# Attention of 32 heads as float32 products of whole operands, two heads side by side on TensorE, in a kernel with two mixture-of-experts layers behind it

## The chip, the core and the metric

The kernel runs on one core of a Trainium2 chip, as one launch. The core has five engines that the text names: TensorE (PE: matrix products; its weight loads are listed apart as PEld), VectorE (DVE), ScalarE (ACT), GpSimd (POOL) and SyncE (SP), which here only issues DMAs. TensorE reads SBUF and writes PSUM; GpSimd works on SBUF alone. The metric is the device time of one execution in microseconds; the median of the runs counts. Every engine works through its own instructions in the order in which the program was written out, and waits where a semaphore tells it to.

## What is computed

Attention over 4 batches of 8 heads, with 576 tokens of 64 numbers each; then a top-1 layer of 8 experts on the 2304 tokens of 512 numbers, then a second such layer, all in float32.

```python
def _attn_ref(q, k, v, tau):
    scale = 1.0 / np.sqrt(q.shape[-1])
    scores = scale * np.matmul(q, k.transpose(0, 1, 3, 2))
    thresh = np.max(scores, axis=-1, keepdims=True) - tau
    scores = np.where(scores >= thresh, scores, -1000000000.0)
    scores = scores - np.max(scores, axis=-1, keepdims=True)
    attn = np.exp(scores)
    attn = attn / (np.sum(attn, axis=-1, keepdims=True) + 1e-09)
    return np.matmul(attn, v).astype(np.float32)
...
x = attn_out.transpose(0, 2, 1, 3).reshape(B * S, H * D)
x = _moe_ref(x=x, **moe_kwargs)          # expert of the largest cosine with expert_emb
return _moe2_ref(x=x, **moe2_kwargs)     # expert of the largest x @ w_gate
# each: out = gate * (relu(x[mask] @ w1[e]) @ w2[e]), e by e
```

## The kernel before

The program has two parts, one after the other. `Attn` does the 32 heads in 16 pairs (heads A and B of a pair); `Moe` then does the two layers of experts. The change touches `Attn` alone.

**The work of a pair.** A head's 576 query tokens are four tiles of 128 rows and 64 tokens left over; the leftovers of both heads share a ninth row tile, R. Row tiles 0 to 3 are of head A, 4 to 7 of head B, 8 is R. For each row tile `scores` (L290) makes 128x576 scores in a PSUM tile `S` of two banks (two buffers), and `least` (L308) scales and negates them into SBUF on VectorE and takes the row's least. Then a row tile goes one of two ways. Five of the nine in a pair between the first and the last two (`MASK_LAST`, L134) take the exponential on ScalarE at once (`exp all`, L342) and are masked afterwards by one VectorE instruction that also makes the row's sum (`mask`, L347). The other four get 1e30 where the score is beyond the bound (`beyond`, VectorE, L322), which GpSimd adds to the scores (`add`, L327) before ScalarE's exponential. `bound` (L317) is a small GpSimd sum per two row tiles.

The probabilities are then transposed by TensorE in units (`unit_t`, L361): a head's 512 tokens by 128 keys (four units) or 64 keys (the fifth), and two units for R. The units, multiplied with the values and summed over the keys (`unit_av`, L414), give 64 values by 512 tokens in the PSUM tile `av`. `out_copy` (L436) brings that to SBUF, `out_rows` (L442) turns it into rows of tokens with the head's part of the router's logits, and `out_scale` (L454) divides by the sums and sends the rows to DRAM.

**Products of parts.** A product is not taken of the float32 numbers as they are. Every operand is split into a high part (ScalarE copies it into the shorter float32r format) and a low part (the difference, on VectorE or GpSimd), and the parts' products are summed in PSUM, each a float32r product. For the scores, queries and keys are split (`hi`, `copy`, `lo`, L244 to L268), and eight or more DMAs per pair (`put`, L270) lay the parts out so that [qh; ql] meets [kh; kh] in one product of 128 rows and qh meets kl in a second. For the values, `values_hi` and `values_lo` (L223, L228) split the values, and `unit_hi` and `unit_lo` (L378, L403) every unit; a unit's low part is made by GpSimd for the units named in `POOL_LO`, after another copy by ScalarE (`unit_copy`, L398), and by VectorE for the rest. Two places have undivided float32 products already: the scores of the first pair (L298), and the one unit of a pair named in `NATIVE` (L129), whose product takes 64 of TensorE's 128 columns (L429).

**What sets the order.** `ops` (L480) lists every step of all pairs with its engine, an assumed duration, what it needs and which buffers it takes. `schedule` (L69) plays them through: an engine that is free takes its ready step with the lowest number from the table `PRIO` (L37) plus 9 per pair. The instructions are then written out by the planned start. So the steps of a pair's scores lie among those of the values of the pair before. Steps have names such as `av B3`; the durations in the listing are the planner's and not the chip's.

Of the kernel before, what the change touches and what calls it, by code (L numbers as in the profile page):

```python
# [36 lines left out]
PRIO = {'warm': -10000, 'add': (-0.16, -0.16, -34.65), 'av A0': (-64.69, -36.16, -74.17), 'av A1': (91.89, 55.73, 39.12), 'av A2': (11.55, -7.69, -15.93),  # L37
        'av A3': (-7.31, -19.57, 3.89), 'av A4': (29.52, 7.73, 37.81), 'av B0': (-101.89, -32.26, -71.6), 'av B1': (1.15, -3.58, 51.29), 'av B2': (27.87, 57.62, 70.32),
        'av B3': (16.24, 19.49, -11.83), 'av B4': (-65.09, -76.86, -45.68), 'av R4': (-52.77, -109.13, -78.47), 'beyond': (-27.93, -27.93, -68.77),
        'bound': (32.21, -8.27, -34.63), 'cpk': (-26.19, -26.19, -9.74), 'cpq': (-78.84, -78.84, -72.62), 'emb norm': 63.12, 'emb put': 185.35, 'emb t': -26.7,  # L40
# [4 lines left out]
        'keys first': 6.99, 'ld w1': 9875.33, 'ldk': (-19.25, -19.25, -6.75), 'ldq': (-40.12, -40.12, -34.25), 'ldv': (-1.36, -19.35, -1.74),  # L45
# [3 lines left out]
        'loq': (24.41, 24.41, 13.42), 'mask': (42.11, 16.85, 52.98), 'out copy A': (2.77, -32.01, -26.34), 'out copy B': (-7.87, 4.44, 9.13),  # L49
        'out copy R': (4.59, -18.98, -47.96), 'out rows A': (-58.69, 8.96, 16.81), 'out rows B': (48.05, 22.06, 57.31), 'out rows R': (100.98, 70, 72.19),  # L50
        'out scale A': (58.37, 23.19, 48.16), 'out scale B': (-22.09, -8.89, 10), 'out scale R': (16.66, -68.73, 5.62), 'params': -3.56,
        'put kh': (-34.17, -34.17, -52.2), 'put qh': (-125.91, -125.91, -110.79), 'put ql': (-46.61, -46.61, -81.72), 'queries A': -1.77, 'queries B': -31.15,
        'raw A0': -5.76, 'raw A2': (-19.29, -23.07, -16.97), 'raw A3': (-21.66, -5.31, -11.85), 'raw B2': (-27.43, -44.98, -62.27), 'raw B3': (17.51, 21.04, 11.67),
        'route add': (-28.79, -28.79, -28.09), 'route argmax': (-42.73, -42.73, -64.14), 'route count': (-101.52, -101.52, -16.14), 'route perm': (5.63, 5.63, -18.58),
        'route prefix': (6.1, 6.1, -7.24), 'route slots': (11.96, 11.96, 28.01), 'scores': (4.78, 0.94, 6.14), 'sign': 38.43, 't A0': (-33.6, 6.93, 4.21),
# [65 lines left out]
class Attn:  # L121
    """Attention of the 32 heads, in pairs; rows of values, and logits of the first router, go to DRAM.

    Of a pair of heads A, B, token 4 p + t stands at row p of tile t; the last 64 tokens of both share tile R.
    Scores are three products of exact parts: [qh; ql] [kh; kh] and qh kl; R takes those of both heads, with zeros between.
    Probabilities are masked after the exponential or before it, transposed, and split like the others.
    """
    UNITS = [(h, k) for h in 'AB' for k in range(5)] + [('R', 0), ('R', 4)]  # of a pair's transposed probabilities
    # in the first pair, those between, the last but one, the last  # L129
    NATIVE = [('A', 1)], [('A', 1)], [('A', 1), ('B', 1)], [('A', 1), ('B', 1), ('A', 2)]  # units whose product with the values is a float32 one  # L130
    # units whose low part GpSimd makes
    POOL_LO = [('A', 3), ('B', 3), ('B', 2), ('A', 2)], [('A', 3), ('B', 3), ('B', 2), ('A', 2)], [('A', 3), ('B', 3), ('B', 2), ('A', 2), ('A', 0)], [('A', 3), ('B', 3), ('B', 2)]
# [74 lines left out]
    def emb_put(s): s.nc.vector.tensor_copy(s.ie[:, :, 64:72], s.pe)  # L207
# [272 lines left out]
    def ops(s, params, done):  # L480
        O = []
# [649 lines left out]
```

## Time and profile before

| what | value |
|---|---|
| median of three runs (1127.10 to 1131.44) | 1127.37 us |
| span of the profiled execution | 1131.5 us |
| its instructions | 17365 |
| first and last `least` of the attention | start at 11.5 and 406.8 us |
| last copy of `av`, the end of the attention's products | starts at 425.0 us |
| TensorE busy, of the span | 957.3 us (85%) |
| VectorE | 713.7 us (63%) |
| ScalarE | 543.9 us (48%) |
| GpSimd | 502.5 us (44%) |

The profile is one execution on the chip. Its span runs from the first to the last instruction; of the three timed runs the slowest, 1131.44 us, is nearest to it, and the median lies 4.1 us below. A group of instructions is named by line, engine, operation and the program's tiles (`out<-in`), with the shape; behind it stand the number of instructions, their time together and the mean of one, then the idle time of the engine before them and who ended it. A record of TensorE runs from the entry of the first column to the end of the last, so that successive records overlap: the distance of their starts, not the length of one, is what a product costs. A product of undivided float32 operands leaves two records. "128x512" at the end of a TensorE group is its output, and 128*64 before it says that 128 rows and 64 columns of the array take part.

### The profile page before, as it was taken

The page shows a single profiled execution, that of the slowest core. Times are in us where ns is not written, and L with a number is a line of the kernel's source. Part 1 is how long each engine was busy: PE and PEld are TensorE (multiplying, and loading weights), DVE is VectorE, ACT ScalarE, POOL GpSimd, SP SyncE. Part 2 cuts the span into 40 slices and gives each one's busy share as a digit, 9 for nine tenths or more (in the row PEclk, how much of TensorE's full clock was granted, in tenths as well). Part 3 has the DMA queues.
Part 4 walks back from the last instruction along what each step waited for, and adds up shares of the span by engine and source line. Part 5 has one row for each costly group of instructions (what it writes and reads, how often), then busy time and mean ns, then how long its engine had stood idle before and what let it go on. Part 6 is the DMA issues. An engine that isn't in the chain of part 4 may idle for free. (4 is left out here: it accounts for less than half of the span.)

```text
span 1131.5 us, 17365 instructions
## 1 busy us (share of the span) xinstructions
PE 957.3 (85%) x5685; PEld 831.9 (74%) x5685; DVE 713.7 (63%) x1611; ACT 543.9 (48%) x1019; POOL 502.5 (44%) x551
## 2 busy tenths in 40 slices
PE   7889899987997995897898798968589898879774
PEld 5777677776786774797787787967578887679673
DVE  7899999999798974563566365435434434344430
ACT  5788768875695772452355243322233322333420
POOL 5687768865686653332343334113313322132321
PEclk9999989998897995988999898989699999996998
DMA  6565646644344022644464444214435433364400
GB/s 161 127 146 125 147 107 149 150 116 95 84 110 96 21 68 61 190 123 139 153 188 137 130 156 137 86 46 152 138 102 195 138 105 118 100 198 149 154 17 24
DMA packets 119527, 136.83 MB, mean 121 GB/s; under 512 B 74869, under 2 KB 78965, under 8 KB 119168
## 3 DMA queue, kind: packets, MB, share of 16 engines
q1 hardware_dynamic: 111648, 109.30, 35.5%
q0 software_dynamic: 7520, 23.90, 6.1%
q14 instruction: 274, 2.24, 0.8%
q8 instruction: 85, 1.39, 0.5%
HBM read 95.40 MB, written 16.68 MB: 99 GB/s over the span
## 5 line engine op out<-in xcount | busy, mean ns | idle before, releaser
L851 PE MATMUL l1p<-xh,w1h 128*128 128x256 f32 (+7 forms) x576 | 190.9, 331 | 82.1 <-issue 53.4
L851 PEld LDWEIGHTS l1p<-xh,w1h 128*128 128x128 f32 x576 | 123.2, 214 | 89.5 <-issue 75.6
L851 PE MATMUL l1p<-xl,w1h 128*128 128x256 f32 (+7 forms) x576 | 185.2, 321 | 0.0
L851 PE MATMUL l1p<-xh,w1l 128*128 128x256 f32 (+7 forms) x576 | 184.9, 321 | 0.0
L854 ACT ACTIVATE hh<-l1p 128x256 fp32r<-128x256 f32 (+7 forms) x144 | 57.9, 403 | 191.0 <-PE l1p L851 146.2
L861 PE MATMUL yps<-w2h,hh 128*128 128x512 f32 x344 | 140.2, 408 | 0.0
L861 PE MATMUL yps<-w2l,hh 128*128 128x512 f32 x344 | 134.5, 391 | 0.0
L861 PE MATMUL yps<-w2h,hl 128*128 128x512 f32 x344 | 134.5, 391 | 0.0
L784 DVE TENSOR_TENSOR w2l<-rw,w2h 128x1024 fp32r<-128x1024 f32 x48 | 74.3, 1559 | 94.7 <-issue 42.3
L784 POOL TENSOR_TENSOR w1l<-rw,w1h 128x1024 fp32r<-128x1024 f32 x17 | 50.6, 2975 | 173.4 <-ACT w1h L783 156.5
L851 PEld LDWEIGHTS l1p<-xl,w1h 128*128 128x128 f32 x576 | 123.4, 214 | 0.0
L851 PEld LDWEIGHTS l1p<-xh,w1l 128*128 128x128 f32 x576 | 123.0, 214 | 0.0
L313 DVE TENSOR_SCALAR_CACHE_REDUCE sn<-psS,nsc 128x576 f32<-128x576 f32 x144 | 114.6, 809 | 12.9 <-PE psS L302 6.9
L783 ACT ACTIVATE w2h<-rw 128x1024 fp32r<-128x1024 f32 x64 | 66.0, 1052 | 109.1 <-PE yps L861 53.4
L370 PE MATMUL pt<-ident,p 128*128 128x128 f32 (+1 forms) x640 | 98.5, 287 | 14.0 <-DVE h L412 8.7
L856 DVE SCALAR_TENSOR_TENSOR hl<-l1p,hh 128x256 fp32r<-128x256 f32 (+7 forms) x144 | 62.8, 446 | 69.4 <-ACT hh L854 64.0
L412 POOL TENSOR_TENSOR lo<-raw,hi 128x512 fp32r<-128x512 f32 x64 | 86.5, 1352 | 32.0 <-ACT raw L401 31.6
L329 POOL TENSOR_TENSOR b<-sn,b 128x576 f32<-128x576 f32 x57 | 84.2, 1479 | 32.7 <-DVE b L325 29.9
L370 PEld LDWEIGHTS pt<-ident,p 128*128 128x128 f32 (+1 forms) x640 | 76.0, 141 | 29.4 <-DVE h L412 11.3
L350 DVE SCALAR_TENSOR_TENSOR p<-sn,th,b 128x576 f32<-128x576 f32 x87 | 94.5, 1091 | 1.0 <-ACT b L345 0.8
L393 ACT ACTIVATE hi<-pt 128x512 fp32r<-128x512 f32 x109 | 63.1, 596 | 38.0 <-PE pt L370 36.7
L345 ACT ACTIVATE b<-sn,nm 128x576 f32<-128x576 f32 x87 | 67.5, 776 | 18.0 <-DVE sn L313 16.2
(253 smaller groups left out, 2176.7 us busy)
## 6 DMA issues: line engine op xcount, KB each, us to landing
rw<-in_moe_w_dram SPq DMA_DIRECT2D x128, 512.0 KB, 4.2
KA<-kh SPq DMA_DIRECT2D x30, 144.0 KB, 4.8
KB<-kh SPq DMA_DIRECT2D x30, 144.0 KB, 2.6
rawk<-in_k_dram SPq DMA_DIRECT2D x16, 256.0 KB, 3.5
rawq<-in_q_dram SPq DMA_DIRECT2D x16, 256.0 KB, 3.7
rawv<-in_v_dram SPq DMA_DIRECT2D x16, 256.0 KB, 3.2
xs<-xb SPq DMA_DIRECT2D x16, 256.0 KB, 3.1
sA<-qh SPq DMA_DIRECT2D x15, 144.0 KB, 2.6
```

What stands on the lines that cost most here:

```text
L313: s.nc.vector.tensor_scalar(out=sn, in0=st.pop(('ps', r))[:, 224:800], scalar1=s.scale, scalar2=3e38, op0=ALU.mult, op1=ALU.min, accum_out ...
L329: s.nc.gpsimd.tensor_tensor(out=st['b', r], in0=st.pop(('sn', r)), in1=st['b', r], op=ALU.add)
L345: s.nc.scalar.activation(out=b, in_=st['sn', r], func=AF.Exp, scale=-1.0, bias=s.of(st, 'nm', r))
L350: s.nc.vector.scalar_tensor_tensor(out=p, in0=st.pop(('sn', r)), scalar=s.of(st, 'th', r), in1=st.pop(('b', r)), op0=ALU.is_le, op1=ALU.mu ...
L370: for t in range(4): s.nc.tensor.transpose(pt[0:n, t * 128:t * 128 + 128], st['p', 4 * (h == 'B') + t][:, k * 128:k * 128 + n], s.id)
L393: s.nc.scalar.activation(out=t if o is None else o, in_=pt, func=AF.Copy)
L412: (nc.gpsimd if pool else nc.vector).tensor_tensor(out=lo, in0=pt, in1=hi.bitcast(F32), op=ALU.subtract)
L783: def split_hi(s, W, R, k): s.nc.scalar.activation(out=W[0][k], in_=R[k], func=AF.Copy)
L784: def split_lo(s, W, R, k, eng): eng.tensor_tensor(out=W[1][k], in0=R[k], in1=W[0][k].bitcast(F32), op=ALU.subtract)
L851: s.nc.tensor.matmul(o, s.W1[a][k][:, fs], X[b][:, k, n0:n1], start=(q == 0), stop=(q == 3 * KC - 1))
L856: s.nc.vector.scalar_tensor_tensor(out=s.H[1][f][:, n0:n1], in0=o, scalar=0.0, in1=s.H[0][f][:, n0:n1].bitcast(F32), op0=ALU.max, op1=ALU. ...
L861: s.nc.tensor.matmul(ps, s.H[a][f][:, ts], s.W2[b][f // 2][:, f % 2, :], start=(f == 0 and q == 0), stop=(f == FC - 1 and q == 2))
```

## The change

Operands are no longer split anywhere in the attention. Queries and keys are transposed, copied once (keys by VectorE, queries by ScalarE) and used as they are: `Tq` and `Tk` hold head A in partitions 0 to 63 and head B in 64 to 127. Row tiles are numbered anew: 2t is tile t of head A, 2t+1 of head B. A step `scores t` makes both, and takes both buffers of `S`: for each half of the keys a product of head A, which uses TensorE's rows 0 to 63, and one of head B, which uses rows 64 to 127. For tile R the queries are laid out with zeros, so that one product of 128 rows serves both heads.

With the values, each unit is copied from PSUM once, by ScalarE, and `av k` takes the units of both heads: head A's product uses TensorE's columns 0 to 63 and writes partitions 0 to 63 of `av`, head B's the other half. The values are used as they were loaded. The units of 64 keys became units of 128 with the last 64 keys in their lower half and zeros in the values for the rest. `out_copy` and `out_rows` then work on both heads together: four products of 144 columns take the place of eight of 72.

What falls away: all steps `hi`, `lo`, `raw`, `put`, `vh` and `vl`, and the first pair's own products. New are `cpk` on VectorE, zeros that are set once in the buffers of queries and values, and one more DMA for the queries' last tokens (one less for the values). Six row tiles of a middle pair are masked after the exponential and three before it (`MASK_FIRST`); in the first and the last two pairs all nine after it. The table `PRIO` is replaced by one of times within a pair, with 17 per pair. The part with the experts is untouched.

```diff
+    MASK_FIRST = (), (2, 4, 6), ()
...
+    def copy(s, j, nm):
...
+        if nm == 'q': s.nc.scalar.activation(out=st['Tq'], in_=st['psq'], func=AF.Copy)
+        else: s.nc.vector.tensor_copy(st['Tk'], st['psk'])
...
-                nc.tensor.matmul(o, st['S' + h][:, c:c + 128], st['K' + h][:, ks], start=True, stop=False)
-                nc.tensor.matmul(o, st['H' + h][:, t:t + 128], st['kl'][:, ks], start=False, stop=True)
...
+    def scores(s, j, t):
+        nc, st = s.nc, s.pair[j]
+        q, k = st['Tq'], st['Tk']
+        rr = (2 * t, 2 * t + 1) if t < 4 else (8,)
+        for r in rr: st['ps', r] = s.psS.tile([128, 1024], F32, tag='S', name='psS')
+        for i in range(2):
+            ks = slice(i * 288, i * 288 + 288)
+            for h, r in enumerate(rr):
+                p = slice(64 * h, 64 * h + 64) if t < 4 else slice(0, 128)
+                nc.tensor.matmul(st['ps', r][:, (224, 512)[i]:(512, 800)[i]], q[p, 128 * t:128 * t + 128], k[p, ks], start=True, stop=True)
...
     def unit_copy(s, j, u):
...
+        if u in s.of_pair(s.DVE_COPY, j): s.nc.vector.tensor_copy(t, pt)
+        else: s.nc.scalar.activation(out=t, in_=pt, func=AF.Copy)
...
+    def unit_av(s, j, k):
...
+        if k == 'R':
...
+            for k in range(5):
+                for i in range(2):
+                    p = t[:, 128 * k:128 * k + 128] if k < 4 else r
+                    nc.tensor.matmul(av[64 * i:64 * i + 64], v(i, k), p[:, 64 * i:64 * i + 64], start=(k == 0), stop=(k == 4))
             return
-        i = int(h == 'B')
         if k == 0: st['av'] = s.psA.tile([128, 512], F32, tag='av', name='av')
-        av = st['av']
-        if s.native(j, u): nc.tensor.matmul(av[0:64], st['rawv'][:, i * 320 + k * 64:i * 320 + k * 64 + 64], p, start=False, stop=False)
-        elif k < 4:
-            nc.tensor.matmul(av, v(i, k), p[0], start=(k == 0), stop=False)
-            nc.tensor.matmul(av, v(i, k), p[1], start=False, stop=False)
-        else: nc.tensor.matmul(av, v(i, 4), p, start=False, stop=True)
...
+        for i, h in enumerate('AB'):
+            nc.tensor.matmul(st['av'][64 * i:64 * i + 64], v(i, k), st.pop(('u', (h, k))), start=(k == 0), stop=(k == 4))
...
-                    if r in s.of_pair(s.MASK_LAST, j):
-                        x = op('exp all', j, 'A', .76, step(s.exp_all), [least[r]], r, alloc=['b'])
...
+                    if r not in s.of_pair(s.MASK_FIRST, j):
+                        x = op(f'exp all {r}', j, 'A', .70, step(s.exp_all), [l], r, alloc=['b'])
...
-        caps = dict(S=2, T=2, A=1, M=1, rawk=2, rawq=2, rawv=3, nat=2, kh=2, qh=2, tr=2, kl=2, ql=2, KA=2, SA=2, V=3, sn=4, b=3, P=12, hi=3, lo=3, h4=2, r4=2, rhl=1, avs=2, avsR=1, xb=2)
+        caps = dict(S=2, T=2, A=1, M=1, rawk=2, rawq=2, rawv=3, Tk=2, Tq=2, sn=5, b=3, P=14, u=6, r4=2, avsM=2, avsR=2, xb=2)
```

The first place is TensorE's row of work in the middle of an early pair of the kernel before: one native unit (L429), the transpose of R's unit of 64 keys and those of a head's unit (L367, L370), a unit's two products with the values (L431, L432) and one row tile's scores (L301, L302, head B).

```order
L429 MATMUL av<-raw,rawv 64x512
L367 MATMUL pt<-ident,p 64x128
L431 MATMUL av<-hi,Nv 128x512
L432 MATMUL av<-lo,Nv 128x512
L370 MATMUL pt<-ident,p 128x128 x4
L301 MATMUL psS<-KB,sB_190 128x288
L302 MATMUL psS<-kl,hB_194 128x288
L301 MATMUL psS<-KB,sB_190 128x288
L302 MATMUL psS<-kl,hB_194 128x288
```

The same place of the changed kernel: L321 are the two heads' products of one `av k`, L232 the four products of one `scores t`, L295 the transposes of units (four make one).

```order
L321 MATMUL av<-u,rawv_182 64x512 x2
L232 MATMUL psS<-Tk,Tq 128x288 x4
L295 MATMUL pt<-ident,p 128x128 x8
L321 MATMUL av<-u,rawv_182 64x512 x2
L232 MATMUL psS<-Tk,Tq 128x288 x4
L295 MATMUL pt<-ident,p 128x128 x8
L321 MATMUL av<-u,rawv_182 64x512 x2
L295 MATMUL pt<-ident,p 128x128 x4
```

A row tile's scores were two pairs of float32r products and now share a step of four float32 products with the other head; the values' products of two heads, which stood apart, now stand next to each other, and TensorE goes from half rows (L232) to whole rows (L295) to half columns (L321) and back for every unit.

The second place is VectorE's row in the same pair before: `least` (L313), `mask` (L350), `beyond` (L325), the low parts of units (L412) and the sums' reciprocals (L355, L356).

```order
L350 SCALAR_TENSOR_TENSOR p,sum<-sn,th,b 128x576
L325 TENSOR_SCALAR b<-sn,th 128x576
L412 TENSOR_TENSOR lo<-pt,hi 128x512
L313 TENSOR_SCALAR sn,nm<-psS,nsc 128x576 x2
L412 TENSOR_TENSOR h_1168<-pt,h_1168 64x512
L313 TENSOR_SCALAR sn,nm<-psS,nsc 128x576
L350 SCALAR_TENSOR_TENSOR p,sum<-sn,th,b 128x576
L325 TENSOR_SCALAR b<-sn,th 128x576
```

And in the changed kernel, where the same steps are L239 (`least`), L276 (`mask`), L251 (`beyond`), and L350 scales rows (`out_scale`).

```order
L276 SCALAR_TENSOR_TENSOR p,sum<-sn,th,b 128x576 x2
L239 TENSOR_SCALAR sn,nm<-psS,nsc 128x576 x2
L251 TENSOR_SCALAR b<-sn,th 128x576
L276 SCALAR_TENSOR_TENSOR p,sum<-sn,th,b 128x576
L239 TENSOR_SCALAR sn,nm<-psS,nsc 128x576 x2
L251 TENSOR_SCALAR b<-sn,th 128x576
L276 SCALAR_TENSOR_TENSOR p,sum<-sn,th,b 128x576
L239 TENSOR_SCALAR sn,nm<-psS,nsc 128x576 x2
```

The low parts are gone from between, and `least` comes in twos, one for each head of a score step.

More of the change, by code (lines that the diff above doesn't have):

```diff
@@ new lines @@
+PERIOD = 17.0
+PRIO = {'first': -93.7, 'warm': -10000, 'emb norm': 10.0, 'emb t': 11.0, 'emb put': 12.0, 'params': 0.0, 'sign': 20.0, 'weights': 0.0,
+        'ldk': -24.0, 'ldq': -24.0, 'ldv': -14.0, 'tk': -7.0, 'tq': -6.5, 'cpk': -6.5, 'cpq': -6.0,
+        **{f'scores {t}': 3.2 * t for t in range(5)}, **{f'bound {t}': 3.2 * t + 2 for t in range(5)},
+        **{f'least {r}': 1.6 * r + .5 for r in range(9)}, **{f'exp all {r}': 1.6 * r + 1.2 for r in range(9)}, **{f'mask {r}': 1.6 * r + 2 for r in range(9)},
+        **{f'beyond {r}': 1.6 * r + 1 for r in range(9)}, **{f'add {r}': 1.6 * r + 1.5 for r in range(9)}, **{f'exp {r}': 1.6 * r + 3 for r in range(9)},
+        'inverse': 17.0, **{f't {h}{k}': 16.0 + 2.6 * k + (h == 'B') for h in 'AB' for k in range(5)}, **{f'copy {h}{k}': 16.5 + 2.6 * k + (h == 'B') for h in 'AB' for k in range(5)},
+        't R0': 29.5, 't R4': 30.0, 'copy R0': 30.0, 'copy R4': 30.5, **{f'av {k}': 18.0 + 2.6 * k for k in range(5)}, 'av R': 32.0,
+        'out copy M': 30.0, 'out copy R': 32.5, 'out rows 0': 31.0, 'out rows 1': 32.0, 'out rows R': 33.0, 'out scale 0': 31.5, 'out scale 1': 32.5, 'out scale R': 33.5,
+        'logits': 34.0, 'route argmax': 36.0, 'route prefix': 37.0, 'route count': 38.0, 'route slots': 38.0, 'route perm': 39.0, 'route add': 40.0,
+        'w1 hi': 100.0, 'w1 lo': 101.0, 'ld w1': 102.0}
@@ L217, in load @@
             dma(r[:, :, 0:256], first.rearrange('h (p t) d -> p h (t d)', p=128))
-            for i in range(2): dma(r[i * 64:(i + 1) * 64, :, 256:320], rest.rearrange('h p d -> p h d'))
-        else:
-            dma(raw[:, 0:512].rearrange('p (t h d) -> p t h d', h=2, d=64), first.rearrange('h (p t) d -> p t h d', p=128))
-            dma(raw[0:64, 512:640].rearrange('p (h d) -> p h d', h=2), rest.rearrange('h p d -> p h d'))
-    def values_hi(s, j):
-        st = s.pair[j]
-        st['V'] = s.nv.tile([128, 2, 5, 2, 64], F32R, tag='Nv', name='Nv')
-        s.nc.scalar.activation(out=st['V'][:, :, :, 0, :], in_=st['rawv'].rearrange('p (h t d) -> p h t d', h=2, d=64), func=AF.Copy)
@@ L228, in values_lo @@
-    def values_lo(s, j):
-        st = s.pair[j]
-        v = st['V']
-        s.nc.gpsimd.tensor_tensor(out=v[:, :, :, 1, :], in0=st['rawv'].rearrange('p (h t d) -> p h t d', h=2, d=64), in1=v[:, :, :, 0, :].bitcast(F32), op=ALU.subtract)
+            dma(r[64:128, :, 256:320], rest.rearrange('h p d -> p h d'))
+            return
+        dma(raw[:, 0:512].rearrange('p (t h d) -> p t h d', h=2, d=64), first.rearrange('h (p t) d -> p t h d', p=128))
+        if nm == 'k': dma(raw[0:64, 512:640].rearrange('p (h d) -> p h d', h=2), rest.rearrange('h p d -> p h d'))
+        else:
+            for h in range(2): dma(raw[64 * h:64 * h + 64, 512 + 64 * h:576 + 64 * h], rest[h])
@@ L233, in transpose @@
     def transpose(s, j, nm):
         nc, st = s.nc, s.pair[j]
-        raw = st['raw' + nm]
-        ps, o = s.psS.tile([128, 1024], F32, tag='S', name='psp'), 128 if nm == 'q' else 0
-        for t in range(4): nc.tensor.transpose(ps[:, o + 128 * t:o + 128 * t + 128], raw[:, 128 * t:128 * t + 128], s.id)
-        for c in ((64, 640) if nm == 'q' else (512,)): nc.tensor.transpose(ps[:, c:c + 64], raw[0:64, 512:640], s.id[0:64, 0:64])
-        st['ps' + nm] = ps[:, 64:704] if nm == 'q' else ps[:, 0:576]
@@ L242, in part @@
-    def part(s, j, nm, p): return s.qk.tile([128, 640 if nm == 'q' else 576], F32R, tag=nm + p, name=nm + p)
-    def hi(s, j, nm):
-        st = s.pair[j]
-        st[nm + 'h'] = s.part(j, nm, 'h')
-        s.nc.scalar.activation(out=st[nm + 'h'], in_=st['ps' + nm], func=AF.Copy)
+        raw, n = st['raw' + nm], 128 if nm == 'q' else 64
+        ps = st['ps' + nm] = s.psS.tile([128, 1024], F32, tag='S', name='psp')[:, 0:512 + n]
+        for t in range(4): nc.tensor.transpose(ps[:, 128 * t:128 * t + 128], raw[:, 128 * t:128 * t + 128], s.id)
@@ L414, in unit_av @@
[L414 to L424 removed]
+        n = 128 if u == ('R', 4) else 512
@@ L445, in out_rows @@
[L445 to L452 removed]
+        nc, st, ie = s.nc, s.pair[j], s.ie[:, j % 4].rearrange('p h w -> p (h w)')
@@ L454, in out_scale @@
+        sb = st['avs', 'R' if h == 'R' else 'M']
+        n = 64 if h == 'R' else 128
+        xp = st['xp', h] = s.psM.tile([n, 1 if h == 'R' else 2, 2 * W], F32, tag='m', name='xp')
+        for i in range(xp.shape[1]):
+            t = 0 if h == 'R' else 2 * h + i
+            nc.tensor.matmul(xp[:, i], sb[:, t * 128:t * 128 + n], ie, start=True, stop=True)
     def out_scale(s, j, h):
         nc, st, b, c = s.nc, s.pair[j], j // 4, 2 * D * (j % 4)
-        xp, rs = st.pop(('xp', h)), st['rs']
@@ L520, in ops @@
-            if j == 0: emb.deps.append(put['A'])
+                x = op('t' + nm, j, 'P', .55, step(s.transpose), [ld[nm]], alloc=['S', 'T' + nm], free=['raw' + nm])
+                if nm == 'k': put[nm] = op('cpk', j, 'D', .70, step(s.copy), [x], free=['S'])
+                else: put[nm] = op('cpq', j, 'A', .60, step(s.copy), [x], free=['S'])
+            if j == 0: emb.deps.append(put['k'])
             if j == 2:
@@ new lines, in ops @@
+            for t in range(5):
+                rr = (2 * t, 2 * t + 1) if t < 4 else (8,)
+                last = op(f'scores {t}', j, 'P', 1.0, lambda j=j, t=t: s.scores(j, t), list(put.values()) + [last], t, alloc=['S'] * len(rr), free=[] if t < 4 else ['Tq', 'Tk'])
+                least = [op(f'least {r}', j, 'D', .76, lambda j=j, r=r: s.least(j, r), [last], r, alloc=['sn'], free=['S']) for r in rr]
+                th = op(f'bound {t}', j, 'G', .25, lambda j=j, t=t: s.bound(j, t), least, t)
+                for r, l in zip(rr, least):
@@ L553, in ops @@
                 step = lambda m, a=u, j=j: lambda: m(j, a)
-                rr = {'A': range(4), 'B': range(4, 8), 'R': [8]}[h]
+                rr = {'A': range(0, 8, 2), 'B': range(1, 8, 2), 'R': [8]}[h]
                 small = u == ('R', 4)
-                x = op('t ' + n, j, 'P', .1 if small else .44, step(s.unit_t), [P[r] for r in rr], alloc=['T'], free=['P'] * len(rr) if k == 4 else [])
-                nat, pool = s.native(j, u), s.pool_lo(j, u)
-                tag = {'R0': 'rhl', 'R4': 'r4'}.get(n, 'h4' if k == 4 else 'nat' if nat else 'hi')
```

292 lines of the change are left out of this document (76 added, 216 removed), and 11 rows, old and new, of the table PRIO.

## The prediction

> **What bounds the kernel now.** I read the page's slices first, for where the attention lies, then the busy times of a stretch of it, then its groups of instructions, and last the timeline of single engines.
>
> ```profile
> PE   7889899987997995897898798968589898879774
> DVE  7899999999798974563566365435434434344430
> 50.00:400.00 350.00, 311.33 (x2029) 259.54 (x2027) 326.39 (x688) 258.87 (x508) 254.64 (x277) 0.94 0.48 112
> L313 DVE TENSOR_SCALAR_CACHE_REDUCE sn<-psS,nsc x144: 757/809/819, 11.5 to 406.8; 128x576 f32<-128x576 f32 x144
> ```
>
> Each digit is 28 us of the span. VectorE stands at 8 and 9 tenths for the first 15 slices, which are the attention (the last `least` starts at 406.8 us), and at 3 to 6 after it. The third line gives 350 us from the middle of the attention: TensorE busy 311.33, weight loads 259.54, VectorE 326.39, ScalarE 258.87, GpSimd 254.64, and a granted TensorE clock of 0.94. VectorE's 93% bounds, with TensorE (89% by its overlapping records) close behind. What VectorE does there:
>
> ```profile
> L313 DVE TENSOR_SCALAR_CACHE_REDUCE sn<-psS,nsc 128x576 f32<-128x576 f32 x123 | 97.9, 809 | 10.8 <-PE psS L302 6.7 <-POOL b L329 2.7 <-PE psS L306 0.6
> L350 DVE SCALAR_TENSOR_TENSOR p<-sn,th,b 128x576 f32<-128x576 f32 x70 | 76.4, 1094 | 0.9 <-ACT b L345 0.8
> L325 DVE TENSOR_SCALAR b<-sn,th 128x576 f32<-128x576 f32 x54 | 47.0, 874 | 1.3 <-POOL th L320 0.2
> L412 DVE TENSOR_TENSOR lo<-pt,hi 128x512 fp32r<-128x512 f32 x40 | 27.2, 681 | 1.2 <-ACT hi L393 1.2
> L412 DVE TENSOR_TENSOR h<-pt,h 64x512 fp32r<-64x512 f32 x27 | 18.5, 684 | 2.5 <-ACT h L393 1.7
> L412 DVE TENSOR_TENSOR rhl<-pt,rhl 128x512 fp32r<-128x512 f32 x14 | 9.6, 685 | 0.3 <-ACT rhl L393 0.2
> ```
>
> There are nine `least` (L313) to a pair, so 123 of them are 13.67 pairs, and a pair takes 350 / 13.67 = 25.6 us. This is the number to beat. The mask (L350) has a mean of 1094 ns; the timeline shows why that is no property of the mask:
>
> ```profile
> 109.46 0.82 DVE L350 SCALAR_TENSOR_TENSOR p<-sn,th,b 128x576 f32<-128x576 f32 x1
> 110.21 0.52 DVE L325 TENSOR_SCALAR b<-sn,th 128x576 f32<-128x576 f32 x1
> 111.37 1.47 DVE L350 SCALAR_TENSOR_TENSOR p<-sn,th,b 128x576 f32<-128x576 f32 x1
> 107.61 0.19 POOL L320 TENSOR_TENSOR th<-nm,taup 128x2 f32<-128x2 f32 x1
> 110.80 1.43 POOL L329 TENSOR_TENSOR b<-sn,b 128x576 f32<-128x576 f32 x1 [3.00 <-DVE b L325]
> ```
>
> With GpSimd idle (107.80 to 110.80 us) a mask takes 0.82 and `beyond` 0.52; beside a GpSimd sum the same mask takes 1.47. VectorE's length depends on how busy GpSimd is.
>
> **The change, VectorE.** The low parts go: (27.2 + 18.5 + 9.6) / 13.67 = 4.0 us of a pair. GpSimd loses far more than it keeps:
>
> ```profile
> L329 POOL TENSOR_TENSOR b<-sn,b 128x576 f32<-128x576 f32 x54 | 79.9, 1482 | 30.1 <-DVE b L325 27.3 <-DMA rawv<-in_v_dram 2.0 <-PE av L433 0.4
> L320 POOL TENSOR_TENSOR th<-nm,taup 128x2 f32<-128x2 f32 x54 | 22.9, 423 | 26.2 <-DVE sn L313 25.8
> 7.89 0.74 DVE L254 COPY firstk<-psp 128x576 f32<-128x576 f32 x1
> L355 DVE TENSOR_SCALAR rs<-sum 128x9 f32<-128x9 f32 x13 | 11.4, 876 | 0.2
> L465 DVE TENSOR_TENSOR xb<-xps,rs 128x288 f32<-128x288 f32 x27 | 12.1, 449 | 3.0 <-PE xps L451 2.9
> ```
>
> It has 254.64 / 13.67 = 18.6 us a pair, and keeps three adds of 1.48 and five bounds of 0.42, which is 6.5. So masks and `beyond` come down towards 0.82 and 0.52. VectorE's new pair: nine `least` of 0.81 (7.3), six masks between 0.82 and 1.09 (4.9 to 6.5), three `beyond` between 0.52 and 0.87 (1.6 to 2.6), the keys' copy 0.74, the sums 0.9, two scalings of 0.45: 16.3 to 19.0, and I take 17.5. It would allow 18 us a pair. What is late next is TensorE, or ScalarE.
>
> **ScalarE.**
>
> ```profile
> L393 ACT ACTIVATE hi<-pt 128x512 fp32r<-128x512 f32 x97 | 56.2, 596 | 36.0 <-PE pt L370 34.7 <-POOL lo L412 0.7 <-PE av L431 0.3
> L345 ACT ACTIVATE b<-sn,nm 128x576 f32<-128x576 f32 x70 | 54.3, 776 | 11.7 <-DVE sn L313 10.0 <-DVE p L350 1.5
> ```
>
> Eleven unit copies, the queries' copy and the copy of `av` at about 0.6 (7.8) and nine exponentials at 0.78 (7.0) make 15, with three reads of sums and two small copies about 16, against 258.87 / 13.67 = 18.9 before. It bounds nothing.
>
> **TensorE.** Here the change lives. The distance of starts follows from merged rows: (their length less that of one record) / (records less one).
>
> ```profile
> 122.52 1.04 PE L370 MATMUL pt<-ident,p 128*128 128x128 f32 x8
> L370 PE MATMUL pt<-ident,p x640: 270/273/476, 23.3 to 421.8; 128*128 128x128 f32 x128, 128*64 128x128 f32 x32
> 25.31 1.13 PE L298 MATMUL psS<-firstk,firstR 128*128 128x288 f32 x4
> L298 PE MATMUL psS<-firstk,firstR x4: 406/406/406, 25.3 to 26.0; 128*128 128x288 f32 x4
> 411.20 1.93 PE L429 MATMUL av<-raw,rawv 128*64 128x512 f32 x4
> L429 PE MATMUL av<-raw,rawv x38: 592/592/644, 30.6 to 423.0; 128*64 128x512 f32 x38
> 409.07 0.71 PE L448 MATMUL xpr<-ie,avsR 128*64 128x72 f32 x8
> L448 PE MATMUL xpr<-ie,avsR x128: 226/226/278, 58.0 to 422.5; 128*64 128x72 f32 x128
> ```
>
> A transpose costs (1.04 - 0.27) / 7 = 0.11 us. The first pair's two products of R leave four records, and the 19 native units 38: an undivided float32 product goes through the array in two passes, one behind the other. A pass of 288 costs (1.13 - 0.406) / 3 = 0.24, one of 512 (1.93 - 0.592) / 3 = 0.45, a short one 0.07. The native unit, with half the columns, takes as long per column as the full-width one: half an array saves nothing by itself. Whether the other half works at the same time, no row of this kernel shows; that is the unknown cost. Its ends are two passes for the two heads together (free) and four (nothing gained). I take three, because in every row TensorE starts its products in the order of the program: A's first pass, A's second, B's first, B's second. A's second pass needs A's half and so waits for A's first; B's first stands behind it in the order and starts with it; B's second comes last. A step of the values (2 products) is then 3 passes long, a step of the scores (4 products) 5 instead of 8.
>
> The Trainium skill, "TensorE: Matmul & The Clock Gate", Part 3 on packing small matmuls, says that products in different row or column groups of the array run at the same time, and that they start and end strictly in program order. No run here shows the first; the starts in the rows agree with the second; by both together the sum would be the one below.
>
> Per pair: 55 transposes (10 of queries and keys, 45 of units) 5.9; scores 4 x 5 x 0.24 + 4 x 0.24 for R = 5.8; values 5 x 3 x 0.45 = 6.7; R's values, 20 short passes of which up to half overlap, 0.7 to 1.4, say 1.0; rows, ten passes at half of 0.24, 1.2. Sum 20.6. Then the array's shape changes, which the kernel before does once a pair:
>
> ```profile
> 405.80 0.60 PE L370 MATMUL pt<-ident,p 128*128 128x128 f32 x4
> 406.33 1.07 PE L429 MATMUL av<-raw,rawv 128*64 128x512 f32 x2
> 407.33 0.66 PE L370 MATMUL pt<-ident,p 128*128 128x128 f32 x4
> ```
>
> Four transposes from 405.80 would let the unit start at 406.23, and it starts at 406.33; its two passes would let the next begin at 407.23, and that begins at 407.33: a visit costs 0.2 us. The new pair has ten (four scores, five values, R's values): 2.2. That makes 22.8 at full clock. At the stretch's 0.94 it would be 24.3; TensorE will wait less, so I take 0.97, 23.5. The last term is idle time. A step of scores now takes both buffers of `S`, so it waits for two `least` where one was enough, and queued behind it on TensorE are units that ScalarE waits for. One more `least` on each of four steps would be 3 us a pair at most; the steps between (values, transposes) cover most of it, since VectorE has 17.5 us of work in more than 23. I take 4%: 24.5 us a pair.
>
> The rest costs nothing that I can see: the parts' DMAs leave SyncE's queue, where loads run a pair ahead, and one more load of queries joins it; if that cover failed, it would be some 3 us once. The start of the first scores may shift by 1 or 2 us either way.
>
> **The sum.** 16 x (25.6 - 24.5) = 18 us off the profiled 1131.5, so 1113.5; the profile stands 4.1 above the median of 1127.4, so 1110, and with the start left open I say 1112. Own range of this case: at full clock with 2% idle a pair is 23.3 (1090); at 0.94 with 5% idle 25.6, and if shape changes between half rows and half columns cost half as much again, 26.6 (1092 to 1143; I put the bulk at 1092 to 1135).
>
> **Rivals.**
> *Full overlap:* both heads' passes run side by side from the first, 2 for 2. Scores 4.8, values 4.5, R 0.7: 19.3 with the visits, 19.9 at clock 0.97. VectorE's 17.5 is then close, and the shared `S` buffers bind: 10% idle, 22.1 a pair, 56 us off: 1072 (1062 to 1090). For it: halves share no rows and no columns. Against: the order of starts. The Trainium skill, "TensorEngine Tiling (Array Packing)", Theoretical Speedup, gives up to 2x for operands of 64 or less, which is this sum; no run here shows it.
> *No overlap, slower:* the halves take turns. It decides as soon as B's first pass starts only after A's second has gone through. Scores 36 x 0.24 = 8.7, values 20 x 0.45 = 8.9, R 1.4: 28.3 with visits, 29.2 at 0.97, 29.8 with 2% idle: 67 us on top, 1194 (1175 to 1215). For it: no row shows overlap, and the change then doesn't do what it says; against: the two products name different rows or columns of the array, and no row shows a half waiting for the other.
> *VectorE stays the bound:* if masks stay at 1.09 it needs 19 us, below TensorE's sum in every case; I count it with full overlap.
>
> **Chances.** Three passes 0.50, full overlap 0.27, no overlap 0.23. A measurement of this kernel tells 0.5% (5.6 us) from no change. Faster by more: 0.27 and two thirds of 0.50, 0.60; within, 0.10; slower, 0.23 and the rest of the middle case, 0.30. The range for 8 in 10 leaves out the lower edge of full overlap and most of the case without overlap: 1064 to 1190; signs are mixed in it, and the likeliest case's own range is 1092 to 1135.
>
> **What would show it.** In the changed profile, a step of scores (L232) should leave eight records with starts that pair up: A's second with B's first, 1.2 us from first to last end of column entry, and a step of values (L321) 1.3. Starts 0.24 or 0.45 apart throughout mean no overlap; B's first beside A's first, full overlap. VectorE should fall to about 70% of a pair with masks near 0.85, TensorE rise above 94%. I am wrong if a pair is off 24.5 us with the passes as forecast: then idle time at `S` or shape changes were mis-sized.

## The result, and the profile after

The changed kernel takes 1080.34 us (median of 4 runs, 1079.94 to 1081.43) where the kernel before took 1129.4 beside it (1127.1 to 1132.32): a ratio of 0.956, 95% interval 0.952 to 0.960, or 49 us less. The forecast was 1112. The time lies in the forecast's range, but it is near the price of a rival, full overlap (1072), and not of the likeliest case. The profiled execution has a span of 1078.8 us.

First where the time went. These are the weight loads of the experts' first products, in the kernel before and in the changed one (start of the first and of the last behind the durations):

```profile
L851 PEld LDWEIGHTS l1p<-xh,w1h x576: 186/188/337, 447.1 to 1099.9; 128*128 128x128 f32 x192
```

```profile
L710 PEld LDWEIGHTS l1p<-xh,w1h x576: 186/188/337, 396.3 to 1047.3; 128*128 128x128 f32 x192
```

The experts begin 50.8 us earlier, and from the first of these loads to the last it is 651 to 653 us in both. The two spans differ by 52.7 us, so all but 2 of the gain is the attention's. The page's slices of the changed kernel, 27 us each:

```profile
PE   7999999999999957978888989975888998888984
DVE  5778787787797445636654646453433535343420
PEclk6899999999999959989889889987899999986887
```

The attention is now the first 13 or 14 of them, with TensorE at 9 tenths. And 300 us from its middle (busy time of TensorE, weight loads, VectorE, ScalarE and GpSimd, then the clock):

```profile
50.00:350.00 300.00, 292.86 (x1962) 179.00 (x1964) 239.75 (x631) 192.54 (x368) 93.96 (x170) 1.00 0.26 64
```

TensorE now stands at 97.6% and VectorE at 80%; GpSimd fell to 31%, and the clock is 1.00 where the forecast took 0.97. The groups of that stretch:

```profile
L239 DVE TENSOR_SCALAR_CACHE_REDUCE sn<-psS,nsc 128x576 f32<-128x576 f32 x125 | 98.3, 811 | 18.1 <-PE psS L232 17.4
L276 DVE SCALAR_TENSOR_TENSOR p<-sn,th,b 128x576 f32<-128x576 f32 x87 | 84.7, 982 | 19.0 <-ACT b L271 16.4 <-POOL th L246 1.9
L251 DVE TENSOR_SCALAR b<-sn,th 128x576 f32<-128x576 f32 x37 | 19.2, 519 | 9.4 <-POOL th L246 9.4
L255 POOL TENSOR_TENSOR b<-sn,b 128x576 f32<-128x576 f32 x38 | 60.9, 1602 | 27.7 <-DVE b L251 17.9 <-ACT b L271 9.1 <-ACT avsR L327 0.7
```

The mean of a group stands behind its busy time. 125 `least` are 13.89 pairs, so a pair takes 300 / 13.89 = 21.6 us, against 25.6 before and 24.5 in the forecast. VectorE has 239.75 / 13.89 = 17.3 us of work in it.

The lines that decide between the cases are the steps of TensorE. Merged records of a scores step (L232) and of a values step (L321), each with the row that starts next:

```profile
99.94 1.24 PE L232 MATMUL psS<-Tk,Tq 64*128 64x288 f32 x8
101.12 1.09 PE L295 MATMUL pt<-ident,p 128*128 128x128 f32 x8
...
109.32 1.08 PE L321 MATMUL av<-u,rawv 128*64 128x512 f32 x4
110.33 0.66 PE L295 MATMUL pt<-ident,p 128*128 128x128 f32 x4
```

From start to next start a scores step takes 1.18 us and a values step 1.01. Taken apart by windows inside the values step (the number in brackets counts the records that are running then):

```profile
109.36:109.46 0.10, 0.10 (x2) 1.00 0.73 164
109.90:110.00 0.10, 0.10 (x4) 1.00 0.00 0
```

Two records run from the step's beginning; the (x4) are those two ending and the second two beginning, which overlap as successive records do. So A's first pass and B's first pass go together, and then the second passes: two passes for the two products. The forecast had three.

### The profile page after: what moved, and what is told of

Same layout as the page of the kernel before. It is cut to its first block, busy times and chain, and to the rows that moved or that the text cites. A ratio compares the mean times of both kernels' runs of the same rounds, so it can differ in the third digit from the quotient of the medians.

```text
span 1078.8 us, 16430 instructions
## 1 busy us (share of the span) xinstructions
PE 947.5 (88%) x5603; PEld 750.6 (70%) x5603; DVE 611.6 (57%) x1525; ACT 468.0 (43%) x859; POOL 313.0 (29%) x422
## 5 line engine op out<-in xcount | busy, mean ns | idle before, releaser
L710 PE MATMUL l1p<-xh,w1h 128*128 128x256 f32 (+7 forms) x576 | 194.4, 338 | 72.6 <-issue 44.3
L710 PEld LDWEIGHTS l1p<-xh,w1h 128*128 128x128 f32 x576 | 126.6, 220 | 79.8 <-issue 73.7
L305 ACT ACTIVATE u<-pt 128x512 f32<-128x512 f32 x192 | 104.6, 566 | 67.1 <-PE pt L295 66.1
L239 DVE TENSOR_SCALAR_CACHE_REDUCE sn<-psS,nsc 128x576 f32<-128x576 f32 x144 | 113.3, 811 | 26.0 <-PE psS L232 25.3
L710 PEld LDWEIGHTS l1p<-xl,w1h 128*128 128x128 f32 x576 | 126.8, 220 | 0.0
L232 PE MATMUL psS<-Tk,Tq 64*128 64x288 f32 (+1 forms) x576 | 110.9, 447 | 5.6 <-DVE sn L239 4.5
L276 DVE SCALAR_TENSOR_TENSOR p<-sn,th,b 128x576 f32<-128x576 f32 x105 | 99.9, 963 | 24.1 <-ACT b L271 19.8
L295 PEld LDWEIGHTS pt<-ident,p 128*128 128x128 f32 x640 | 69.8, 142 | 49.5 <-issue 39.2
L271 ACT ACTIVATE b<-sn,nm 128x576 f32<-128x576 f32 x105 | 80.2, 773 | 42.8 <-DVE sn L239 42.7
L321 PE MATMUL av<-u,rawv 128*64 128x512 f32 x320 | 96.4, 615 | 0.7 <-ACT u L305 0.7
L295 PE MATMUL pt<-ident,p 128*128 128x128 f32 x640 | 94.1, 283 | 2.2 <-ACT u L305 1.3
```

The lines of the kernel that those rows point to most:

```text
L232: nc.tensor.matmul(st['ps', r][:, (224, 512)[i]:(512, 800)[i]], q[p, 128 * t:128 * t + 128], k[p, ks], start=True, stop=True)
L239: s.nc.vector.tensor_scalar(out=sn, in0=st.pop(('ps', r))[:, 224:800], scalar1=s.scale, scalar2=3e38, op0=ALU.mult, op1=ALU.min, accum_out ...
L271: s.nc.scalar.activation(out=b, in_=st['sn', r], func=AF.Exp, scale=-1.0, bias=s.of(st, 'nm', r))
L276: s.nc.vector.scalar_tensor_tensor(out=p, in0=st.pop(('sn', r)), scalar=s.of(st, 'th', r), in1=st.pop(('b', r)), op0=ALU.is_le, op1=ALU.mu ...
L295: for t in range(4): s.nc.tensor.transpose(pt[:, t * 128:t * 128 + 128], st['p', 2 * t + (h == 'B')][:, ks(k)], s.id)
L305: else: s.nc.scalar.activation(out=t, in_=pt, func=AF.Copy)
```

## The experiments

The theory after this profile: the two halves of the array work independently, and the attention is bound by TensorE, whose steps the overlap keeps short. The rivals: the forecast's own (products start in program order), and that the overlap matters little and the gain is VectorE's and GpSimd's relief from splitting. Ratios below are to the kernel before; the changed kernel's is 0.956.

### Both products without overlap

```diff
-  matmul(av[64*i : 64*i+64], v(i, k), u(h, k), start=(k == 0), stop=(k == 4))
+  # a values tile holds, for each k: v of A, 64 columns of zeros, v of B
+  matmul(av, tile[:, k*192 + i*64 : k*192 + i*64 + 128], u(h, k), start=(k == 0 and i == 0), stop=(k == 4 and i == 1))
-  matmul(S of r, q[64*h : 64*h+64, tile t], k[64*h : 64*h+64, ks])
+  matmul(S of r, tq[h][:, tile t], k[:, ks])      # tq[h]: zeros in the other head's rows
```

> Both heads' operands are padded with zeros to the whole array (queries of each head in a tile of its own with zeros in the other head's rows, values of each head between zero columns, both heads summed into the same 128 rows of av), so no two products can run side by side; results are the same. Theory (halves work independently, TensorE bounds the attention): a scores step goes from 1.18 us to eight passes of 0.24 = 1.92, a values step from 1.01 to four of 0.45 = 1.80; per pair 4 x 0.74 + 5 x 0.79 = 6.9 us more, 16 pairs 110 us, so about 1190 us. Rival (the gain came from VectorE and GpSimd being rid of the splitting, the overlap is worth little): within 10 us of 1080.

Measured: 1150.86 us, ratio 1.018 (1.012 to 1.024). Without the overlap the change makes the kernel slower, by 1.8%. A values step, a scores step and what starts behind it:

```profile
121.75 1.88 PE L330 MATMUL av<-u,rawv 128*128 128x512 f32 x4
123.47 2.10 PE L240 MATMUL psS<-Tk,tq 128*128 128x288 f32 x8
125.41 1.04 PE L303 MATMUL pt<-ident,p 128*128 128x128 f32 x8
```

The values step from the inside:

```profile
121.80:121.90 0.10, 0.10 (x1) 1.00 0.00 0
```

A values step is now 1.72 us and a scores step 1.94, with one record running at a time. The same eight and four passes took 1.18 and 1.01 side by side, so the halves bring a factor of 1.64 and 1.70 (the Trainium skill, "TensorEngine Tiling (Array Packing)", Theoretical Speedup, says up to 2x; the rows agree with that bound). The rival of the relief alone falls. But 71 us came where 110 were expected (in the profiles the experts start at 468.3 us instead of 396.3). TensorE's time per pair by what it works on, from each row's start to the next row's and summed over 50 to 350 us, shows why:

```
us a pair              changed   no overlap
values (av)             5.42       8.41
scores (psS)            6.14       8.90
R's values (avR)        0.86       0.71
unit transposes (pt)    6.14       5.22
q, k transposes (psp)   1.25       1.42
rows, routing           1.76       1.80
sum, the pair          21.6       26.5
```

Values and scores grow by 5.8 us, not 6.9. A pass of 512 took 0.43 and not 0.45, and many of the changed kernel's steps were longer than 1.01 and 1.18 (24 of 55 values steps and 10 of 55 scores steps in the stretch). And 0.9 us of the transposes' time goes away, which in the changed kernel was waiting. The 97.6% of "busy" TensorE contains waits.

### One product at a time without overlap

> Only the values are padded (each values step takes the whole array); scores as changed. Theory of independent halves: 5 x 0.79 = 4.0 us a pair more, 63 us, about 1143. Theory of the forecast (products start in program order, so a values step is three passes already): 5 x 0.45 = 2.2 us a pair, 36 us, about 1116. Rival (only VectorE's relief counts): about 1080.

Measured: 1119.32 us, 0.989 (0.983 to 0.994): 37 us on the changed kernel by the ratios. By the time alone this is the forecast's theory, and that would be the wrong reading: that theory needs the changed kernel's values step to be three passes of 0.43, 1.29 us, and its usual step is 1.01 (31 of the 55). Some steps are 1.32 (16 of them), since B's product starts later than A's. One of those in the changed kernel:

```profile
102.14 1.39 PE L321 MATMUL av<-u,rawv 128*64 128x512 f32 x4
103.46 1.24 PE L232 MATMUL psS<-Tk,Tq 64*128 64x288 f32 x8
```

Inside that step of the changed kernel:

```profile
102.16:102.30 0.14, 0.14 (x1) 1.00 1.28 287
102.50:102.60 0.10, 0.10 (x2) 1.00 0.80 177
```

One record runs at first, and a second joins it at 102.46, while A's first pass is still going. The trace shows what that second one waited for, the copy of B's unit on ScalarE:

```profile
101.81 0.60 ACT L305 ACTIVATE u<-pt 128x512 f32<-128x512 f32 x1 [2.25 <-PE pt L295]
```

It ended at 102.41. So the longer steps are a late operand and not an order that TensorE keeps.

> Only the scores are padded (whole array each; ScalarE copies the queries in three pieces, about 0.7 us more a pair); values as changed. Theory of independent halves: 4 x 0.74 = 3.0 us a pair more, 47 us, about 1127. The forecast's three-pass theory gives nearly the same (eight passes for five, 0.72 a step). Rival (only VectorE's relief counts): about 1080.

Measured: 1111.95 us, 0.982 (0.976 to 0.987): 29 us by the ratios. By the start of the experts in the profiles, values alone cost 40.6 us and scores alone 31.8, which is 72.4 together where both at once cost 72.0. Each costs less than its steps' growth, for the reasons above.

### The same products in another order

```diff
-  for i in range(2):                # half of the keys
-      for h, r in enumerate(rr):    # head
+  for h, r in enumerate(rr):
+      for i in range(2):
```

> The same scores products in another order: both of head A, then both of head B, instead of alternating. Theory of independent halves, each with its own queue: a step stays at 1.18 us and the time within 0.5% of 1080. Theory of starts in program order: A's four passes come before B's first, of which only A's last can overlap: seven passes, 1.7 us and a visit, 0.6 us a step more, 2.4 us a pair, 38 us, about 1118. If TensorE can look only a product ahead, between the two.

Measured: 1077.05 us, 0.950 (0.945 to 0.956), the same as the changed kernel within the intervals; the experts of its profile start at 396.7 us, 0.4 from the changed kernel's 396.3. A step of it, in which A's two products stand ahead of B's first in the program, with the row behind it:

```profile
107.57 1.25 PE L232 MATMUL psS<-Tk,Tq 64*128 64x288 f32 x8
108.75 0.66 PE L295 MATMUL pt<-ident,p 128*128 128x128 f32 x4
```

The step's beginning:

```profile
107.60:107.70 0.10, 0.10 (x2) 1.00 0.00 0
```

1.18 us again, and two records from the beginning. If A's second product had to start before B's first could, a single record would run for the first 0.48 us. The Trainium skill, "TensorE: Matmul & The Clock Gate", Part 3, has matmuls start and end strictly in program order; these rows differ, and the measurement decides. This settles the forecast's failed step.

### More work for TensorE, for VectorE, for both relieved engines

> The changed kernel with one transpose more in each of a pair's ten large units (the unit's first transpose is done twice into the same place), so 10 x 0.11 = 1.1 us of TensorE a pair that no one needs; nothing else is added. Theory (TensorE bounds the attention now): 16 x 1.1 = 18 us more, about 1098. Rival (VectorE or the S buffers bound it, TensorE's busy share is waiting): within 4 us of 1080.

Measured: 1088.85 us, 0.961 (0.957 to 0.964), some 5 us more by the ratios, and the two intervals overlap; in the profiles the experts start 9.0 us later. That is between a third and half of the 18 that were added. TensorE is not the bound in the plain sense: its steps need about 19.4 us of a pair (45 x 0.11, 5 x 1.01, 0.73, 4 x 1.18, 0.97, and 3.0 of q, k, rows and routing), and some of the 2.2 that are left took up the added work.

> The changed kernel with six subtractions of 128x512 in SBUF (about 0.68 us each, 4.1 us a pair) more on VectorE, which is what the splitting cost it before; no one waits for them but what stands behind them on VectorE. Theory (TensorE bounds, VectorE has 21.6 - 17.3 = 4.3 us of slack a pair): up to 1 us a pair, 1080 to 1096. Rival (the gain is VectorE's relief): 4.1 us a pair, 65 us, about 1145.

Measured: 1106.1 us, 0.976 (0.974 to 0.979): 23 us more, outside the expected range on the upper side and far below 65. VectorE goes to 93%, with 4.1 us a pair added where 4.3 were free; the stretch first:

```profile
50.00:350.00 300.00, 278.16 (x1808) 170.75 (x1806) 278.60 (x658) 178.66 (x338) 113.93 (x160) 0.97 0.26 63
```

And the groups of its masks and of the added subtractions:

```profile
L286 DVE SCALAR_TENSOR_TENSOR p<-sn,th,b 128x576 f32<-128x576 f32 x77 | 91.4, 1197 | 2.4 <-ACT b L281 2.0
L239 DVE TENSOR_TENSOR sv<-sv 128x512 f32<-128x512 f32 x75 | 51.3, 684 | 0.2
```

A mask is 1197 ns now, from 982. With six masks that is another 1.3 us a pair, so VectorE got 5.4 us more where 4.3 were free; the expectation had left the masks as they were. That this is the whole reason isn't shown: a pair took 1.45 us more.

> As the run with six subtractions on VectorE, and eight of 128x512 on GpSimd as well (about 1.36 us each, 10.9 a pair), so both engines carry again what they had before, and the overlap of TensorE's halves stays. Theory: VectorE has 17.3 + 4.1 and masks that lengthen beside GpSimd's work (0.82 to about 1.1, 6 of them, and the added subtractions likewise), 23.5 to 25 us a pair: VectorE bounds again, 1110 to 1135. If the overlap alone made the gain: 1080 to 1096, as without GpSimd's work.

Measured: 1173.07 us, 1.037 (1.033 to 1.040), slower than the kernel before, and 38 us over the upper end of the expectation. The group of the added subtractions shows them almost twice as long:

```profile
L239 DVE TENSOR_TENSOR sv<-sv 128x512 f32<-128x512 f32 x67 | 82.4, 1230 | 1.0
```

They read SBUF twice, which the kernel before's low parts, from PSUM, did not; so the next run gave the old work back in a form nearer to the old one.

```diff
+  # for k < 3 of both heads, behind ScalarE's copy u of the unit pt; holds pt and u until done
+  nc.vector.tensor_tensor(out=scratch, in0=pt, in1=u, op=ALU.subtract)
+  # eight times a pair
+  nc.gpsimd.tensor_tensor(out=sg[:, 0:512], in0=sg[:, 0:512], in1=sg[:, 512:1024], op=ALU.subtract)
```

> Another try at giving both engines their old work back: for six of a pair's units VectorE subtracts ScalarE's copy from the transposed unit in PSUM (128x512, what it did for the low parts in the kernel before, 0.68 us each) into a place that no one reads, and holds the unit's bank and its product until it has; GpSimd does eight subtractions of 128x512 in SBUF that no one needs (1.3 us each). The six subtractions read PSUM, which in the kernel before kept them at 0.68 us beside GpSimd's work; the SBUF ones of the run before this took 1.23. Theory (the gain needs both, the overlap and the relief): VectorE 17.3 + 4.1 and masks lengthened from 0.98 to about 1.1, 22.5 to 24 us a pair, 1095 to 1120. If the overlap alone made the gain: within 10 us of 1080. If the slowdown of the run before this was the work itself and not the lengthened SBUF subtractions: about 1170 again.

Measured: 1157.29 us, 1.022 (1.017 to 1.027): again slower than before, and above the expectation. ScalarE's waits for units in 300 us, of this kernel and then of the changed one:

```profile
ACT u L317 <- PE pt L306: 102.0, 66, 6.2
```

```profile
ACT u L305 <- PE pt L295: 57.1, 59, 2.6
```

Two things come together, and this run doesn't part them: VectorE is 87% busy (262.07 of 300 us) with longer masks (1173 ns), and the two banks of units are held longer, so that ScalarE waits for units nearly twice as much. No engine is full: TensorE is busy for 271.54 of the 300 us, and which wait sets the pace stays open. What the run does show is that the overlap alone does not make the gain: with the overlap in place and work of the old kind and size given back, the gain is gone. It isn't the old work itself, so the price of the relief alone is not measured.

### The first pair's clock, and another order

In the changed kernel TensorE idles from 7.3 to 10.5 us (its last product before that starts at 7.0), and the clock is 0.50 from 10 to 33 us; scores steps of the first pair leave 2.3 to 3.0 us of records. Five microseconds of it (the clock is the third number from the end):

```profile
20.00:25.00 5.00, 3.76 (x12) 2.31 (x10) 4.60 (x12) 2.23 (x3) 0.20 (x1) 0.50 0.15 32
```

> The changed kernel with TensorE products that no one needs (128x128 of the identity, into the bank of av) while it waits in the first pair: 14 behind the first transposes, 6, 6, 4, 4, 4 ahead of the five scores steps. In the changed kernel the granted clock is 0.50 from 10 to 30 us, after TensorE idles from 6.8 to 10.5. Theory: the clock stays up, steps of 2.3 to 3.0 us come down to 1.2, and 3 to 8 us go: 1072 to 1077. Rival (VectorE's two least a step set the first pair's pace): within 2 us of 1080.

Measured: 1076.93 us, 0.951 (0.948 to 0.953). The same five microseconds:

```profile
20.00:25.00 5.00, 4.71 (x27) 3.08 (x27) 4.38 (x13) 2.60 (x4) 0.39 (x2) 1.00 0.21 47
```

The clock is 1.00, the first pair's steps came down to 1.2 to 2.0 us, and the profile's experts begin at 393.1 us instead of 396.3. 3 us are what the profiles show; the intervals overlap, so the times alone don't show it.

```diff
-  MASK_FIRST = (), (2, 4, 6), ()
+  MASK_FIRST = (), (1, 2, 6), ()
-  op(f'scores {t}', j, 'P', 1.0, ...
+  op(f'scores {t}', j, 'P', 1.17 if t < 4 else 1.0, ...
-  op(f'least {r}', j, 'D', .76, ...
+  op(f'least {r}', j, 'D', .81, ...
...
+  PERIOD and PRIO: found by a search for the shortest attention under these durations
```

> The changed kernel with the same instructions in another order: the planner's durations set to what the trace of the changed kernel shows (scores 1.17, values 1.05, least 0.81, mask 0.90, sum 1.55, unit copy 0.57 us) and its table of due times searched for the shortest attention under them; tiles 1, 2 and 6 are masked before the exponential instead of 2, 4 and 6. Theory (of a pair's 21.6 us TensorE's steps need 19.5, and 2.1 are waits inside and between steps that the order makes): half to three quarters of the waits go, 1.0 to 1.6 us a pair, 1054 to 1066. Rival (the waits belong to the two S and two T buffers, whatever the order): within 5 us of 1080.

Measured: 1056.77 us, 0.931 (0.928 to 0.935), as the theory of waits had it: 24 us below the changed kernel by the medians, 28 by the ratios. The values steps that took 1.32 are gone (73 of the stretch's steps have a mean of 1.02), and the stretch holds 15 pairs of them, 20.0 us a pair. The stretch, with the instructions on the tile `av` alone (300 records of TensorE, 20 to a pair):

```profile
50.00:350.00 300.00, 81.59 (x300) 15.02 (x300) 8.85 (x15) 0.99 0.28 71
```

Its experts' first product:

```profile
L715 PEld LDWEIGHTS l1p<-xh,w1h x576: 186/188/337, 374.9 to 1024.4; 128*128 128x128 f32 x192
```

Only 14 pairs of `least` lie in the same stretch: VectorE ran further ahead at its beginning. The experts start 21.4 us earlier than in the changed kernel. Most of the waits belonged to the order, not to the number of buffers: of 21.6 us a pair some 1.3 to 1.6 went with the same buffers.

> That order together with the products of no use that keep TensorE's clock at 1.00 in the first pair. Theory: 3 to 6 us below the run without them, 1050 to 1062. Rival (the first pair's pace is VectorE's): no difference between the two.

Measured: 1051.03 us, 0.929 (0.925 to 0.932), the fastest of all. Its profile's experts start at 370.0 us, 4.9 earlier than without the added products, though the two intervals overlap.

## Why the prediction was wrong

**The step that failed:** "I take three, because in every row TensorE starts its products in the order of the program." The rows that supported it were all of products that shared both rows and columns of the array; none could tell an order from a resource that was taken. The changed profile and the run with another order show two passes for two products: a values step takes 1.01 us where three passes and a visit were to take 1.55. In its place: two products that use different rows (scores), or different columns (values), go on by themselves, in the scores at least two products deep.

**What bounds before, and the relief.** Right. VectorE's new pair is 17.3 us (17.5 forecast), `beyond` 0.52, masks 0.98 between the 0.82 and 1.09 given; GpSimd has 93.96 / 13.89 = 6.8 (6.5), ScalarE 13.9 (16). That VectorE would then have slack, and TensorE come up against the end, was right too, though VectorE fell to 80% of a pair and not to 70%, as the pair got shorter, and the masks to 0.98 and not near 0.85. The runs with such work given back show that relief is needed.

**TensorE's sum, term by term.** The forecast's 22.8 us is of steps without waits, and has to be held against the 19.4 that the changed kernel's steps need. Values with their visits: 7.7 forecast, 5 x 1.01 = 5.05 measured, which is most of the difference. Scores with theirs: 6.6 against 4 x 1.18 + 0.97 = 5.7; the step itself hit the forecast's 1.2 by a cancellation, four passes and a visit of 0.2 looking like five passes. R's values 1.2 against 0.73. The other way went the rows with the routing, 1.2 against 1.76, as the sum had no routing. Two slips nearly cancel: 55 transposes of 0.11 are 6.05 and not 5.9, and ten visits of 0.2 are 2.0 and not 2.2.

**Clock and idle time.** 0.97 was forecast and 1.00 granted, worth 0.7 us a pair. The 4% of idle time was 1.0 us; the waits came to 21.6 - 19.4 = 2.2, half of them within the units' transposes (6.14 where the 45 need 4.95). So the steps were 3.4 too long in the forecast and the clock's term 0.7, and the waits 1.2 too short, which makes the 2.9 us a pair between 24.5 and 21.6.

**From pairs to the time.** 16 x 2.9 = 46 us is more than the miss of 32. Most of the rest is in the kernel before: its pair of 25.6 us holds for the stretch from 50 to 400 us, but from its first to its last `least` (11.5 to 406.8 us) a pair takes 24.9. The forecast took the 25.6 for all 16, which made its gain some 11 us too large and hid as much of the miss. In the changed kernel both ways of counting give 21.6 (`least` from 13.4 to 356.0). The first `least` came 1.9 us later than before, as allowed for, but the half clock up to 33 us was not foreseen; the run that keeps the clock up prices it at 3 us.

**The rivals.** *Full overlap* was right in mechanism and near in size: 22.1 a pair for 21.6, with "10% idle" where the steps' 19.4 of 21.6 leave 10%. The fact named in its favour, that the halves share no rows and no columns, was the better evidence, though it is not exact: the scores' halves share the columns and the values' halves share the rows, and not sharing one of the two was enough. *No overlap* had the right sign: the run that takes the overlap away is slower than before, at 1151 instead of 1194, because products of the whole array need no visits (the values step of that run is four passes of 0.43 and nothing more), the clock stays at 1.00 and the longer steps cover waits.

## What to carry to other kernels

Two float32 products that use different halves of the array, of its rows or of its columns, ran side by side here from their first pass, and for the scores the order between them made no difference. Cost such a pair as the two passes of one product and a visit, and look at the operand that arrives last. A busy share of 97% is not yet a bound: add a known bit of useless work, and see how much of it comes back in the time. After a change of operands, set the planner's durations to the new trace and search its order again; here that was worth about half as much as the change (24 us of 49).

## What the runs showed of the chip

A VectorE mask, which reads SBUF twice, gets longer beside GpSimd, and a subtraction that reads PSUM once and SBUF once does not. In the run with the old work given back, rows of VectorE and of GpSimd around the same time:

```profile
201.06 3.02 POOL L243 TENSOR_TENSOR sg<-sg 128x512 f32<-128x512 f32 x2
201.36 1.59 DVE L287 SCALAR_TENSOR_TENSOR p<-sn,th,b 128x576 f32<-128x576 f32 x1
202.88 0.68 DVE L321 TENSOR_TENSOR sv<-pt,u 128x512 f32<-128x512 f32 x1
203.48 1.22 DVE L287 SCALAR_TENSOR_TENSOR p<-sn,th,b 128x576 f32<-128x576 f32 x1
...
207.01 1.27 POOL L243 TENSOR_TENSOR sg<-sg 128x512 f32<-128x512 f32 x1
207.31 1.29 DVE L262 TENSOR_SCALAR b<-sn,th 128x576 f32<-128x576 f32 x1
...
213.53 0.80 DVE L287 SCALAR_TENSOR_TENSOR p<-sn,th,b 128x576 f32<-128x576 f32 x1
213.75 1.84 POOL L266 TENSOR_TENSOR b<-sn,b 128x576 f32<-128x576 f32 x1 [0.46 <-DVE b L262]
```

Beside GpSimd's two subtractions (201.06 to 204.08) the mask, with two operands in SBUF, took 1.59 us, and the subtraction from PSUM 0.68 as ever. At 213.53 the mask began first and took 0.80, and GpSimd's sum, elsewhere 1.41, took 1.84. The Trainium skill, "SBUF — State Buffer", section "Who interferes with whom", says that a VectorE instruction with two SBUF inputs contends with a GpSimd instruction that reads SBUF, and that one with at most one SBUF input, outside the two-port modes, doesn't; these rows agree. `beyond` (L262), which reads SBUF once, also got longer: 1.29 us beside GpSimd's subtraction at 207.01, where it takes 0.52 alone. So a single read of SBUF is not safe by itself; whether `beyond` runs in such a mode, no row here shows.
